# Attention rebuilt in 64-row halves with float32 q and k, inside a float32 attention and two-MLP kernel

## The chip, the cores and the metric

The kernel runs on one core of a Trainium2 chip. The metric is the device time of one launch in microseconds, the median of three runs; lower is better. One execution is also taken by the hardware profiler, and all rows below come from it.

## The reference, cut to what matters

```
# q, k, v: [2, 12, 448, 64] float32
scores = q @ k.T / sqrt(64); scores above the diagonal = -1e9
attn = exp(scores - rowmax); attn /= attn.sum(-1) + 1e-9
x = (attn @ v) -> [2 * 448, 12 * 64]
xn = x / sqrt(mean(x * x, -1) + 1e-6) * rms_g
g = xn @ w_gate; val = xn @ w_val          # [768, 1536] each
y = (g * sigmoid(g) * val) @ w_out         # [1536, 768]
out = relu(y @ w_in) ** 2 @ w_out2         # [768, 2048], [2048, 768]
```

The five weight matrices arrive as float64, the rest as float32. All results are float32.

## The kernel before, in words

TensorE (PE) does every product. To get float32 accuracy out of fast products, each operand is split into a high and a low float32r part, and three products (high x high, high x low, low x high) are summed in PSUM. For the weights the split costs six steps a chunk of 768 columns: `w_exponent`, `w_sign`, `w_upper`, `w_lower` (float64 words to float32), `w_high`, `w_low` (lines 175 to 213). PSUM has eight one-bank buffers in one pool, `ps_m`.

**Attention, lines 232 to 456.** The unit is a head; two heads (a pair) share a load, with head 0 on partitions 0 to 63 and head 1 on 64 to 127. Queries go in four chunks of CP = 112. For a head: `stack` (L299) issues three DMAs on SP's queue that copy the parts of q and k to both partition halves, so that one 128-row product does two of the three split products; `scores` (L309) does one float32 product for chunk 0 (L319, from the raw q and k) and two float32r products for each other chunk (L329: one of 128 rows with `st`, one of 64 rows with `qkl`); `shift` (L331) masks and scales from PSUM to SBUF and takes the row minimum on VectorE (DVE); `expo` (L346) exponentiates on ScalarE (ACT) and sums the rows with the accumulator; `transpose` (L360) turns the weights, ten 112x112 transposes a head; `split_h` and `split_l` (L376, L390) split them on ACT and DVE; `values` (L394) multiplies by v, whose stationary tiles have zeros in the other head's columns (L408, nine float32r products, and one float32 product L403). The sums' reciprocals make a way through DRAM: `over_sums` (L418) writes them, `spread_sums` (L428) reads them back as rows, and `finish` (L413) multiplies. `square` and `add_square` collect RMSNorm's sums. GpSimd (POOL) rounds and splits q, k (`prep_h`, `prep_l`).

**The order around it.** The programs of all engines are in an order written by hand: `BODY` lists the steps of one head with lags, in four phases, and `run` (L605) emits them. From head 23 on, `solo` steps convert the weights of the first five features of the first MLP (SOLO = 5) and `fill` (L549) puts their products for batch 0, 180 products at L552, one by one between attention's. `norm_step` does RMSNorm for each batch after its heads.

**After attention.** `mlp1` (L651): features 5 to 11 and batch 1 of features 0 to 4, whose weights are loaded and converted a second time; each feature has 36 products of 448 columns a batch (L230 to L232 in `mm3`). Then `layer` (L671) for w_out, w_in and the last weights. From the first of these products on there are 2268.

Of the kernel before, what the change touches and what calls it, by code (L numbers as in the profile page):

```python
# [9 lines left out]
F32R = mybir.dt.float32r  # L10
U32 = mybir.dt.uint32
# [7 lines left out]
CP = 112  # L19
# [5 lines left out]
SOLO = 5  # L25
WARM = 9

QB = 2
THREE = 24
KT = [23, 25, 26, 27, 28, 29, 31, 32, 33, 35, 35, 36]  # L30
I0 = -1
PH = [19, 19, 26]
ENG = {'last': 'AAAA',
 'prep_h': 'PAAP',
 'prep_h0': 'D',
 'prep_l': 'PPPP',
 'radd': 'DDDD',
 'split_h': 'AAAA',
 'sqadd': 'PPPP',
 'square': 'PAAP',  # L40
 'v_h': 'AAAA',
 'v_l': 'DPPP',
 'w_exponent': 'APAA',
 'w_high': 'PAPA',
 'w_low': 'DDPP',
 'w_lower': 'DDDD',
 'w_sign': 'DDPD',
 'w_upper': 'DDDD'}
NORM_H = ['APPPPP', 'AAADDD']
NORM_L = ['PPPPDD', 'PPPPDD']  # L50
START = [['load', 1], ['load', 0], ['prep_h', 0], ['v_h', 0], ['prep_l', 0], ['v_l', 0], ['load', 2]]
BODY = [[['load', -4], ['fill', 8], ['heat', 1], ['scores0', -1], ['stack', -2], ['values', 2], ['expo1', 0],
  ['norm', 0], ['finish', 4], ['v_l', 1], ['expo3', 0], ['w_upper', -2], ['shift0', -1], ['fill', 7],
  ['norm', 0], ['tr0', 0], ['w_low', -3], ['sh1', 1], ['prep_h', -4], ['solo_load', 0], ['solo_done', 4],
  ['load_g', 4], ['w_exponent', 1], ['over_sums', 1], ['norm', 0], ['sh2', 1], ['scores2', -1], ['norm', 0],
  ['sl1', 1], ['fill', 5], ['scores1', -1], ['solo_mms', -1], ['fill', 3], ['sl2', 1], ['w_high', 0],
  ['shift2', -1], ['spread_sums', 2], ['scores3', -1], ['shift1', -1], ['square', 4], ['norm', 0],
  ['heat', 3], ['fill', 1], ['tr2', 0], ['expo0', -1], ['shift3', -1], ['sh0', 0], ['norm', 0],
  ['w_lower', -4], ['v_h', 0], ['w_sign', -2], ['add_square', 5], ['prep_l', -4], ['tr1', 0], ['sl0', 0],
  ['expo2', -1], ['fill', 3], ['norm', 0], ['fill', 4]],  # L60
 [ ['expo1', 0], ['values', 2], ['scores0', -1], ['solo_mms', -2],
  ['sl0', 1], ['norm', 0], ['square', 5], ['sl1', 2], ['fill', 1], ['tr0', 1],
  ['fill', 1], ['prep_l', -3], ['fill', 1], ['fill', 1], ['norm', 0],
  ['tr2', 1], ['prep_h', -4], ['fill', 1], ['spread_sums', 3], ['expo2', 1], ['sh0', 1],
  ['norm', 0], ['fill', 1], ['expo0', 0],
  ['add_square', 5], ['w_exponent', -4], ['over_sums', 2],
  ['shift3', 0], ['scores3', -1], ['norm', 0], ['sh2', 1], ['load', -6], ['sl2', 1],
  ['shift0', -1], ['fill', 1], ['shift2', 0], ['fill', 1], ['norm', 0], ['finish', 4],
  ['fill', 1], ['v_l', 1], ['fill', 1], ['w_low', -2], ['fill', 1], ['fill', 1],
  ['shift1', -1], ['fill', 1], ['expo3', 0], ['stack', -2],  # L70
  ['fill', 1], ['w_high', -5], ['fill', 1],
  ['norm', 0], ['solo_load', -7], ['w_upper', -4], ['w_lower', -2],
  ['solo_done', 2], ['scores1', -1],
  ['v_h', 0], ['tr1', 0], ['fill', 1], ['fill', 1],
  ['fill', 1], ['w_sign', 0], ['fill', 1], ['fill', 1],
  ['scores2', -1], ['sh1', 0],
  ['norm', 0], ['fill', 0]],
 [['shift1', 0], ['norm', 0], ['v_l', 1], ['expo3', 0], ['finish', 4],
  ['solo_load', -4], ['add_square', 6],
  ['norm', 0], ['fill', 1], ['norm', 0], ['fill', 1], ['w_lower', -2],  # L80
  ['w_sign', -3], ['sh1', 1], ['load', -5], ['fill', 1], ['tr2', 1],
  ['scores3', -1], ['expo0', 0], ['fill', 1], ['fill', 1], ['values', 2],
  ['norm', 0], ['fill', 1], ['stack', -3], ['w_high', -2],
  ['sh0', 1], ['norm', 0], ['prep_l', -3], ['spread_sums', 3], ['shift2', 0],
  ['sh2', 1], ['expo1', 0], ['over_sums', 2], ['solo_mms', -1], ['prep_h', -5], ['w_low', -2],
  ['norm', 0], ['fill', 1], ['scores0', -1], ['scores1', -1],
  ['fill', 1], ['fill', 1], ['scores2', -1], ['sl0', 1], ['expo2', 0],
  ['fill', 1], ['sl2', 1],
  ['v_h', 0], ['solo_done', 1], ['square', 5], ['fill', 1], ['tr0', 0],
  ['w_exponent', -4], ['norm', 0], ['shift3', -1], ['sl1', 1],  # L90
  ['tr1', 0], ['w_upper', -3],
  ['shift0', -1], ['fill', 0]],
 [ ['scores3', -2], ['fill', 1], ['fill', 1],
  ['w_lower', -2], ['fill', 1], ['sh1', 0], ['tr1', 0], ['w_high', -2],
  ['w_sign', -3], ['norm', 0], ['fill', 1], ['prep_h', -5], ['norm', 0],
  ['shift0', -2], ['over_sums', 1], ['finish', 4], ['w_upper', -3], ['scores1', -2], ['prep_l', -4],
  ['solo_done', 2], ['expo1', 0], ['fill', 1],
  ['square', 5], ['norm', 0], ['solo_mms', -1],
  ['fill', 1], ['sh0', 0], ['w_low', -2], ['fill', 1], ['norm', 0],
  ['shift3', -1], ['sl1', 1], ['fill', 1], ['norm', 0], ['sl0', 1], ['tr0', 0],  # L100
  ['expo3', -1], ['spread_sums', 1], ['values', 1], ['fill', 1], ['sl2', 1],
  ['solo_load', -5],
  ['sh2', -1], ['fill', 1], ['w_exponent', -4], ['fill', 1],
  ['fill', 1], ['fill', 1], ['add_square', 5], ['stack', -2], ['norm', 0], ['fill', 1],
  ['v_h', 0], ['expo2', -2], ['tr2', -1], ['shift2', -2],
  ['scores0', -1], ['load', -5], ['shift1', -2], ['fill', 1],
  ['v_l', 0], ['scores2', -2],
  ['norm', 0], ['expo0', -1], ['fill', 0]]]
NORMPOS = [[124, 127, 135, 137, 138, 142, 144, 143, 143, 150, 152, 152, 155, 143, 155, 158, 157, 160, 167, 166, 170, 174], [215, 222, 229, 241, 243, 246, 249, 256, 275, 275, 250, 299, 308, 295, 311, 315, 313, 326, 348, 326, 333, 342]]


@with_exitstack
def tile_attention_moe_moe2(ctx: ExitStack, tc: tile.TileContext, qk, v, wg, wv, wo, w2i, w2o, rms_g, out):
    """float32 throughout: every product's operands are split exactly into two float32r parts
    (12 significant bits each) and the products of the parts are summed in float32 PSUM.

    qk     [B * NPAIR, P, 2, S]  q and k of each pair of heads, transposed
    v      [B * NPAIR, CP, NCH, 2, D]
    wg, wv [NF1, P, NCC, 2 * P]  stationary tiles, contraction on partitions: float64's words
    wo     [NCC, P, NF1, 2 * P]  # L120
    w2i    [NF2, P, NCC, 2 * P]
# [34 lines left out]
    def EP(name):  # L156
        return E(ENG[name][cur_phase[0]])

# [140 lines left out]
    def stack(u):  # L299
        if u < 2:  # L300
            return
# [449 lines left out]
```

## Time and profile before

| | us |
|---|---|
| median of three runs | 764.91 |
| the three runs | 749.92, 775.11, 764.91 |
| profiled execution: from its first to its last instruction | 733.1 |
| PE busy in it | 694.9 |
| DVE busy | 496.0 |
| POOL busy | 292.4 |
| ACT busy | 156.1 |

The page gives the profiled execution's span, and no time around it: between its span and the three runs' times lie 16.8 to 42.0 us, 31.8 to the median. PE's busy time is not time at its peak: products are pipelined, and an array that runs at the lower of its two clock levels is as busy as one at the higher. PEclk is the granted clock as a share of 2.4 GHz; 0.5 is 1.2 GHz.

### The profile page before, as it was taken

To read this page: it belongs to the slowest core of one execution; us is meant where nothing else is said; L and a number is where in the kernel's file an instruction comes from. 1 tells how busy PE (TensorE), PEld (TensorE's weight loads), DVE (VectorE), ACT (ScalarE), POOL (GpSimd) and SP (SyncE) were. 2 spreads that over 40 slices of the span, in tenths; PEclk is the share of its full clock that TensorE was granted. 3 is DMA by queue.
4 is the path that set the end of the run, shared out by engine and by line. 5 is a ranking of instruction groups with operands and counts; after the bars stand their busy time and mean duration, and the time that the engine had idled before them with its cause. 6 is when DMAs were issued, how large, how long until landed. Compare 5 with 4: busy or idle time off the path is not lost.

```text
span 733.1 us, 8884 instructions
## 1 busy us (share of the span) xinstructions
PE 694.9 (95%) x3199; PEld 589.7 (80%) x3199; DVE 496.0 (68%) x799; ACT 156.1 (21%) x409; POOL 292.4 (40%) x282
## 2 busy tenths in 40 slices
PE   7899898999888888999999899999999999999998
PEld 3566566677677777999997799999999999999997
DVE  5447346447859998888799977557888887445510
ACT  3546346445623300000000000001111110000000
POOL 4322323328666543433454432215565544222210
PEclk6859659559998999999999999999999999999999
DMA  6678977697774224334244454333232323443200
GB/s 163 96 110 109 154 105 115 119 163 104 125 170 143 89 79 147 118 109 151 87 129 138 162 174 133 127 91 125 87 129 87 111 83 109 147 139 120 82 26 25
DMA packets 34860, 85.82 MB, mean 117 GB/s; under 512 B 14400, under 2 KB 20288, under 8 KB 34816
## 3 DMA queue, kind: packets, MB, share of 16 engines
q1 hardware_dynamic: 34816, 85.26, 46.5%
q8 instruction: 25, 0.41, 0.3%
q14 instruction: 19, 0.16, 0.1%
HBM read 72.35 MB, written 2.80 MB: 103 GB/s over the span
## 4 chain that ended last, share of the span: by engine, by line
PE 69%; DVE 12%; DMA 12%; issue 3%; POOL 2%; SPq 1%; ACT 1%; DVEq 0%; POOLq 0%; ACTq 0%
PE py L232 15%; PE py L231 15%; PE py L230 15%; PE s L329 6%; DMA st<-qkl 4%; PE o L408 4%; PE ta L367 3%; DMA wraw<-in_wv 3%; DVE wt L198 3%; DMA rd<-r 2%; DVE wt L203 2%; PE pv L232 2%; DVE wraw L194 2%; PE pv L231 2%; PE pv L230 2%
## 5 line engine op out<-in xcount | busy, mean ns | idle before, releaser
L161 POOL TENSOR_SCALAR whl<-wt 128x768 fp32r<-128x768 f32 (+1 forms) x72 | 66.9, 930 | 111.3 <-PE py L232 93.4
L211 DVE TENSOR_TENSOR whl<-wt,whl 128x768 fp32r<-128x768 f32 (+1 forms) x68 | 67.5, 992 | 48.4 <-POOL whl L161 48.2
L340 DVE CUSTOM_DVE_ANT_0 sm<-s,mask 112x224 f32<-112x224 f32 (+2 forms) x96 | 42.2, 447 | 75.4 <-PE s L329 67.5
L184 POOL TENSOR_SCALAR wt<-wraw 128x768 f32<-128x768 f32 (+1 forms) x68 | 62.7, 922 | 74.4 <-DVE whl L211 46.3
L203 DVE SCALAR_TENSOR_TENSOR wt<-wraw,wt 128x768 uint32<-128x768 uint32 (+1 forms) x80 | 84.5, 1058 | 1.3
L198 DVE SCALAR_TENSOR_TENSOR wt<-wt,wraw 128x768 uint32<-128x768 uint32 (+1 forms) x80 | 81.7, 1022 | 2.3
L194 DVE TENSOR_SCALAR wraw<-wt 128x768 uint32<-128x768 uint32 (+1 forms) x75 | 50.2, 671 | 39.6 <-POOL wt L184 34.1
L232 PE MATMUL py<-y,whl 128*128 128x448 f32 x192 | 70.4, 367 | 0.0
L230 PE MATMUL py<-y,whl 128*128 128x448 f32 x192 | 70.4, 367 | 0.0
L231 PE MATMUL py<-y,whl 128*128 128x448 f32 x192 | 70.4, 366 | 0.0
L232 PE MATMUL py<-hh,whl 128*128 128x448 f32 x192 | 70.1, 365 | 0.0
L230 PE MATMUL py<-hh,whl 128*128 128x448 f32 x192 | 70.1, 365 | 0.0
L231 PE MATMUL py<-hh,whl 128*128 128x448 f32 x192 | 70.1, 365 | 0.0
L351 ACT ACTIVATE p<-sm,nb 112x224 f32<-112x224 f32 (+2 forms) x96 | 50.8, 529 | 44.5 <-DVE nb L340 43.1
L232 PE MATMUL py<-h,whl 128*128 128x448 f32 x144 | 53.3, 370 | 2.4 <-DVE whl L211 2.4
L161 POOL TENSOR_SCALAR hh<-hh 128x448 fp32r<-128x448 f32 x32 | 35.1, 1098 | 49.1 <-DVE hh L698 48.7
L230 PE MATMUL py<-h,whl 128*128 128x448 f32 x144 | 53.3, 370 | 0.0
L231 PE MATMUL py<-h,whl 128*128 128x448 f32 x144 | 53.3, 370 | 0.0
L552 PE MATMUL pg<-x,whl 128*128 128x448 f32 x180 | 46.0, 408 | 7.1 <-POOL whl L211 5.8
L161 POOL TENSOR_SCALAR qkh<-qkraw 128x896 fp32r<-128x896 f32 x11 | 10.6, 961 | 96.3 <-DMA qkraw<-in_qk 52.6
L552 PEld LDWEIGHTS pg<-x,whl 128*128 128x128 f32 x180 | 37.2, 212 | 13.2 <-POOL whl L211 7.5
L232 PE MATMUL pv<-x,whl 128*128 128x448 f32 x114 | 42.7, 374 | 3.4 <-DVE whl L211 3.4
(107 smaller groups left out, 1434.6 us busy)
## 6 DMA issues: line engine op xcount, KB each, us to landing
wraw<-in_wg SPq DMA_DIRECT2D x17, 768.0 KB, 4.4
wraw<-in_wv SPq DMA_DIRECT2D x17, 768.0 KB, 4.3
wraw<-in_w2i SPq DMA_DIRECT2D x16, 768.0 KB, 4.2
wraw<-in_wo SPq DMA_DIRECT2D x12, 768.0 KB, 4.3
wraw<-in_w2o SPq DMA_DIRECT2D x12, 640.0 KB, 4.1
qkraw<-in_qk SPq DMA_DIRECT2D x11, 448.0 KB, 10.1
st<-qkh SPq DMA_DIRECT2D x22, 224.0 KB, 7.5
wraw<-in_w2o SPq DMA_DIRECT2D x6, 768.0 KB, 4.5
```

The costliest lines, as they stand in the source:

```text
L161: eng.tensor_scalar(o, i, 1.0, 1.0, ALU.mult, ALU.mult)
L184: eng.tensor_scalar(e["t"], hi, 2.0 ** -112, 1.0, ALU.mult, ALU.mult)
L194: nc.vector.tensor_scalar(e["s"], e["t"].bitcast(U32), 0x80000000, None, ALU.bitwise_and)
L198: nc.vector.scalar_tensor_tensor(u, u, 3, e["s"], ALU.logical_shift_left, ALU.bitwise_or)
L203: nc.vector.scalar_tensor_tensor(u, lo, 29, u, ALU.logical_shift_right, ALU.bitwise_or)
L211: eng.tensor_sub(e["hl"][:, 1, :n], e["t"].rearrange("p (k n) -> p k n", n=P), e["hl"][:, 0, :n].bitcast(F32))
L230: nc.tensor.matmul(ps, w[:, 0, i], x[:, 0], start=first and i == 0, stop=False)
L231: nc.tensor.matmul(ps, w[:, 0, i], x[:, 1], start=False, stop=False)
L232: nc.tensor.matmul(ps, w[:, 1, i], x[:, 0], start=False, stop=last and i == n - 1)
L329: nc.tensor.matmul(h["s"][c][:, o:o + nn], a, b, start=i == 0, stop=i == len(terms) - 1)
L351: nc.scalar.activation(p, h["m"][c], AF.Exp, bias=h["nb"][:, c:c + 1], scale=-1.0, accum_out=e["sums"][:, u % 2, c:c + 1])
L552: nc.tensor.matmul(o, w, xs[0][i][:, part], start=st_, stop=sp_)
```

## The change

Attention is written anew, and everything in it is emitted by a list scheduler in Python (`Order`) that keeps a model of each engine's time: each step has a due time, the engines that may do it with a cost for each, the steps it follows and the buffers it takes; the step that can start first goes next.

The unit is now a pair. Queries go in chunks of 128 (the last has 64), both heads of a pair in one step: head 0 on PE's rows 0 to 63, head 1 on rows 64 to 127, one product after the other (`sc`). q and k stay float32 and are neither split nor copied; the causal mask is added by bf16 products of constants into PSUM. The scores of a pair lie in two PSUM buffers (`s1`, `s2`, two banks each, and there are two such buffers in all). DVE takes the maxima straight from PSUM (`mx`), ACT exponentiates from PSUM with the scale in the instruction, POOL multiplies the weights by 1/sum while the queries still are on partitions (`ml`; nothing goes through DRAM), PE transposes, ACT or DVE copies to SBUF, and `values` does float32 products, head 0 on PE's columns 0 to 63 and head 1 on 64 to 127. The second product of sums with x is gone: `finish` is a copy.

Features 0 to 2 of the first MLP (NE = 3, six chunks of weights) are converted during attention and kept; their products for batch 0 (108) are steps with due time 1000, so they go where PE has nothing else. After attention come batch 1 of those three features, then features 3 to 11 for both batches: 2340 products. `mm3`, `load_w`, `gated` and `layer` stay.

```diff
-CP = 112
+CP = 64
-SOLO = 5
...
+NE = 3
+STRIDE = 5.0
+SLACK = 0.1
+SWITCH = 0.18
...
+    ps_s = att.enter_context(tc.tile_pool(name="ps_s", bufs=2, space=PSUM))
+    ps_t = att.enter_context(tc.tile_pool(name="ps_t", bufs=1, space=PSUM))
+    ps_o = att.enter_context(tc.tile_pool(name="ps_o", bufs=1, space=PSUM))
+    ps_n = att.enter_context(tc.tile_pool(name="ps_n", bufs=1, space=PSUM))
...
+    order = Order(dict(qk=3, v=NV, s=2, p1=2, p2=2, t=1, pt=2, o=1, n=1, x=9, sq=1, ssq=1, raw=2, wt=3, whl=3,
+                       early=3, tt=2, tu=2, hh=2))
...
+        def sc(buf, o, c, new):
+            def f(e):
...
+                s, n = z[buf], P * (c + 1)
+                qs = slice(c * P, (c + 1) * P)
+                for h in range(2):
+                    nc.tensor.matmul(s[:, h, o:o + n], z["qk"][BOTH[h], 0, qs], z["qk"][BOTH[h], 1, :n],
+                                     start=True, stop=False)
+                for k in range(2):
+                    for h in range(2):
+                        nc.tensor.matmul(s[:, h, o + n - P + k * D:o + n], both[BOTH[h], k], both[BOTH[h], 2 + k, k * D:],
+                                         start=False, stop=k == 1)
...
+        def sc3(e):
...
+            for i, h in ((0, 0), (1, 1), (1, 0), (0, 1)):
+                nc.tensor.matmul(s[BOTH[h], i, 256:480], z["qk"][BOTH[h], 0, qs],
+                                 z["qk"][BOTH[h], 1, i * 224:(i + 1) * 224], start=True, stop=i == 0)
+            for h in range(2):
+                nc.tensor.matmul(s[BOTH[h], 1, 416:480], both[BOTH[h], 0, :D], both[BOTH[h], 2, :D],
+                                 start=False, stop=True)
...
+                if k == 6:
+                    nc.vector.tensor_reduce(z["mx"][:, 6:7], src, mybir.AxisListType.XY, ALU.max)
+                else:
+                    nc.vector.tensor_reduce(z["mx"][:, k:k + 2], src, AX, ALU.max)
...
+                nc.scalar.activation(out_, src, AF.Exp, bias=z["nb"][:, k:k + 1], scale=SC,
+                                     accum_out=z["su"][:, k:k + 1])
...
+        for k, (buf, h, o, n, dst) in enumerate((
+                ("s1", 0, 0, 128, "p1"), ("s1", 1, 0, 128, "p1"), ("s1", 0, P, 384, "p1"), ("s1", 1, P, 384, "p1"),
+                ("s2", 0, 0, 256, "p2"), ("s2", 1, 0, 256, "p2"), ("s2", 0, 256, 448, "p2"))):
...
+                E(e).tensor_scalar(t, t, z["r"][:, k:k + 1], 1.0, ALU.mult, ALU.mult)
...
+            for i in range(4):
+                nc.tensor.transpose(z["t2"][:, 0, i * P:(i + 1) * P], z["p2"][:, 0, i * P:(i + 1) * P], ident)
...
+            for j in range(4):
+                n = S - j * P
+                for h in range(2):
+                    nc.tensor.matmul(z["o"][BOTH[h], j * P:S], z["v"][:, j, h * D:(h + 1) * D],
+                                     z["pt"][:, h, KO[j]:KO[j] + n], start=j == 0, stop=j == 3)
...
+        def finish(e):
+            z["x"] = xrp.tile([P, S], F32, tag="xr", name="xr")
+            copy(e, z["x"], z["o"][:, :S])
...
+        for p in range(NPR):
+            step(p)
+        norm(0, (NPAIR + 2.5) * STRIDE)
+        norm(1, 0.0)
+        for k in range(2 * NE):
+            ahead_steps(k, (5 + 0.9 * k) * STRIDE)
+        for ft in range(NE):
+            ahead_products(ft, 1000.0 + ft)
...
+    for ft in range(NE):
+        mlp1(ft, ahead[2 * ft]["hl"], ahead[2 * ft + 1]["hl"], 1)
+    for ft in range(NE, NF1):
+        g, u = load_w(wg[ft], NCC), load_w(wv[ft], NCC)
         for b in range(B):
             mlp1(ft, g, u, b)
-    for ft in range(SOLO):
-        g, u = load_w(wg[ft], NCC), load_w(wv[ft], NCC)
-        mlp1(ft, g, u, 1)
```

A pair's steps after the change, per kind: ten float32 products for scores (six of 128, 256 and 384 columns, four of 224), 14 bf16 products for masks, 16 transposes, eight value products (448, 320, 192 and 64 columns a head); four maxima over 256, 768, 512 and 448 columns; seven exponentials and seven multiplications over 1984 columns; five copies over 2496 columns; one square and one addition over 448.

## Rows read from the trace of the kernel before

**Rows 1.** Windows: length, busy us (count) PE, PEld, DVE, ACT, POOL; PEclk; DMA; GB/s
```profile
0.00:251.00 251.00, 226.80 (x931) 162.22 (x932) 153.70 (x381) 114.36 (x332) 109.00 (x90) 0.78 0.72 129
...
251.00:319.00 68.00, 61.69 (x288) 54.48 (x287) 59.62 (x73) 5.37 (x11) 29.48 (x31) 0.97 0.33 111
...
319.00:733.00 414.00, 406.39 (x1984) 372.98 (x1982) 282.69 (x347) 36.34 (x67) 153.89 (x162) 1.00 0.34 111
```

**Rows 2.** Windows cut where the granted clock changes, columns as in rows 1
```profile
33.30:53.80 20.50, 18.30 (x54) 12.22 (x55) 8.29 (x26) 7.63 (x25) 6.21 (x5) 0.53 0.85 134
...
53.80:77.70 23.90, 23.17 (x122) 16.17 (x121) 16.51 (x52) 15.47 (x51) 5.51 (x5) 0.97 0.81 117
...
77.70:108.40 30.70, 27.82 (x83) 18.70 (x84) 12.65 (x38) 11.10 (x36) 10.19 (x9) 0.52 0.81 118
...
108.40:128.90 20.50, 18.01 (x95) 12.52 (x94) 12.53 (x40) 12.07 (x39) 8.71 (x7) 0.97 0.79 126
...
128.90:163.00 34.10, 34.10 (x111) 23.92 (x111) 14.82 (x50) 13.48 (x42) 10.20 (x9) 0.52 0.80 136
```

**Rows 3.** Timeline of PE: start, us, engine, line, operation [idle before <-releaser]
```profile
35.51 0.59 PE L329 MATMUL s<-st 128*112 128x336 f32 x1 [2.51 <-DMA st<-qkl]
...
80.58 0.59 PE L329 MATMUL s<-st 128*112 128x336 f32 x1 [3.61 <-DMA st<-qkl]
...
128.59 0.38 PE L329 MATMUL s<-st 128*112 128x336 f32 x1 [2.49 <-DMA st<-qkl]
```

**Rows 4.** Timeline of PE, one head at the lower and one at the higher level
```profile
40.13 0.71 PE L319 MATMUL s<-qkraw 64*112 64x112 f32 x2
...
40.77 2.33 PE L408 MATMUL o<-pt,vz 112*128 112x448 f32 x6
...
49.66 0.71 PE L319 MATMUL s<-qkraw 64*112 64x112 f32 x2
...
112.14 0.45 PE L319 MATMUL s<-qkraw 64*112 64x112 f32 x2
...
112.52 1.33 PE L408 MATMUL o<-pt,vz 112*128 112x448 f32 x6
...
114.58 0.55 PE L367 MATMUL ta<-ident,p 112*112 112x112 f32 x4
...
114.89 0.39 PE L329 MATMUL s<-st 128*112 128x336 f32 x1
...
115.21 0.41 PE L329 MATMUL s<-qkl,st 64*112 64x336 f32 x1
...
117.63 0.45 PE L319 MATMUL s<-qkraw 64*112 64x112 f32 x2
```

**Rows 5.** Groups of instructions, shapes apart: | busy us, mean ns | idle before
```profile
L203 DVE SCALAR_TENSOR_TENSOR wt<-wraw,wt 128x768 uint32<-128x768 uint32 x68 | 74.6, 1099 | 0.9
...
L351 ACT ACTIVATION_READ_ACCUMULATOR p<-sm,nb 112x1 f32 x96 | 18.2, 190 | 0.0
...
L351 ACT ACTIVATE p<-sm,nb 112x448 f32<-112x448 f32 x24 | 16.1, 669 | 13.1 <-DVE nb L340 13.1
...
L340 DVE CUSTOM_DVE_ANT_0 sm<-s,mask 112x448 f32<-112x448 f32 x24 | 15.0, 623 | 12.0 <-PE s L329 11.3 <-ACT p L351 0.7
...
L454 POOL TENSOR_TENSOR ssq<-ssq,sq 128x448 f32<-128x448 f32 x10 | 13.8, 1378 | 0.0
...
L163 ACT CAST pt<-ta 112x448 fp32r<-112x448 f32 x24 | 12.7, 530 | 36.0 <-PE ta L367 35.9
...
L161 POOL TENSOR_SCALAR qkh<-qkraw 128x896 fp32r<-128x896 f32 x11 | 10.6, 961 | 96.3 <-DMA qkraw<-in_qk 52.6 <-DMA st<-qkl 15.8 <-DMA vraw<-in_v 10.7
...
L422 DVE TENSOR_SCALAR r<-sums 112x8 f32<-112x8 f32 x12 | 6.6, 550 | 0.0
...
L449 POOL TENSOR_TENSOR sq<-xr 128x448 f32<-128x448 f32 x7 | 6.5, 934 | 0.0
...
L478 PE MATMUL rb<-dg,ones 112*128 112x112 f32 x16 | 3.2, 362 | 0.2 <-DVE dg L473 0.2
```

More of the change, by code (lines that the diff above doesn't have):

```diff
@@ L24 @@
 NPAIR = H // 2
-SOLO = 5
 WARM = 9
[L28 to L108, printed above, removed]
@@ L428, in spread_sums @@
-    def spread_sums(p):
-        e = pairs[p]
-        d = e["rd"]
-        rb = e["rb"] = at.tile([P, S], F32, tag="rb", name="rb")
-        for i in range(2):
-            row = d[i].rearrange("c p -> (c p)").unsqueeze(0).to_broadcast([D, S])
-            nc.sync.dma_start(out=rb[i * D:(i + 1) * D], in_=row)
-    ssqs = []
-    def square(p):
-        e = pairs[p]
+    ps_s = att.enter_context(tc.tile_pool(name="ps_s", bufs=2, space=PSUM))
+    ps_t = att.enter_context(tc.tile_pool(name="ps_t", bufs=1, space=PSUM))
@@ new lines, in tile_attention_moe_moe2 @@
+    both = atc.tile([P, 4, P], BF16, name="both")
+    nc.vector.tensor_copy(both, half)
+    NV = 3
+    vt = []
+    for i in range(NV):
+        t = atc.tile([P, 4, 2 * D], F32, name=f"vt{i}")
+        nc.gpsimd.memset(t[D:, 3], 0.0)
+        vt.append(t)
+    p2t = []
+    for i in range(2):
+        t = atc.tile([P, 2, 512], F32, name=f"p2t{i}")
+        nc.gpsimd.memset(t[:, 1, S:], 0.0)
+        p2t.append(t)
+    L3 = 1408
+    KO = (0, S, 896, 1344)
+    order = Order(dict(qk=3, v=NV, s=2, p1=2, p2=2, t=1, pt=2, o=1, n=1, x=9, sq=1, ssq=1, raw=2, wt=3, whl=3,
+                       early=3, tt=2, tu=2, hh=2))
@@ L440, in square @@
         b = p // NPAIR
+        z["bx"], z["fi"] = bx, fi
         if p % NPAIR == 0:
[L442 to L454 removed]
@@ L579, in tile_attention_moe_moe2 @@
-    head_f = dict(stack=stack, values=values)
-    for c in range(NCH):
-        for n, f in (("scores", scores), ("shift", shift), ("expo", expo)):
-            head_f[f"{n}{c}"] = lambda u, f=f, c=c: f(u, c)
-    for j in range(3):
-        for n, f in (("tr", transpose), ("sh", split_h), ("sl", split_l)):
-            head_f[f"{n}{j}"] = lambda u, f=f, j=j: f(u, j)
-    pair_f = dict(load=load, prep_h=prep_h, prep_l=prep_l, v_h=v_h, v_l=v_l, over_sums=over_sums, spread_sums=spread_sums,
-                  finish=finish, square=square, add_square=add_square)
@@ L634, in tile_attention_moe_moe2 @@
-    with tc.manual_schedule():
-        heat(WARM)
-        for name, p in START:
-            for q in todo(name, p, NPR):
-                pair_f[name](q)
-        for i in range(I0, NH + 60):
-            cur_phase[0] = sum(i >= q for q in PH)
-            for name, lag in BODY[cur_phase[0]]:
-                run(name, lag, i)
-            if nxt.get("solo_done", 0) == len(solo) and not mms and len(xs[1]) == NCC and nslot[0] > max(NORMPOS[1]):
-                break
+    ahead = [dict() for _ in range(2 * NE)]
@@ new lines, in tile_attention_moe_moe2 @@
+    with tc.manual_schedule():
+        ps = ps_n.tile([P, 512], F32, tag="n", name="warm")
+        for _ in range(WARM):
+            nc.tensor.matmul(ps[:, :256], warm[:, :P], warm, start=True, stop=True)
+        for p in range(NPR):
[6 more added lines that the diff above has]
+            ahead_products(ft, 1000.0 + ft)
+        order.add(30.0, {"S": 2.0}, lambda e: nc.sync.dma_start(out=g_sb, in_=rms_g))
+        order.run()
```

671 lines of the change are left out of this document (353 added, 318 removed).

## The prediction

> **What bounds the kernel now.** I read the windows first, to see which stage the change can touch. The first window ends where `mlp1` begins, at 251 us [rows 1]: attention, both norms and 180 MLP products. From there to the end PE runs 2268 products of one kind in 482 us, at a clock of 0.97 to 1.00; in the last 414 us one takes 406.39 / 1984 = 0.205 us, and PE idles under 2%. That part isn't touched. In the first 251 us PE is busy 226.8 us, but its clock is only 0.78, and no other engine is busy over 154 us. So PE bounds this stage too, and the question is why at a low clock.
>
> Cut at the changes of clock, the stage shows it [rows 2]: the mean is 0.97 in two stretches and 0.52 to 0.53 in three, so PE runs at either 2.4 or 1.2 GHz. In each of the three cases the timeline has an idle PE just before or at the fall, of 2.51, 3.61 and 2.49 us, each waiting for a DMA of `stack` [rows 3]. After it the lower level stays for 20.5, 30.7 and 34.1 us although PE is busy nearly throughout. One head, from one chunk-0 product to the next, costs 49.66 - 40.13 = 9.53 us at 1.2 GHz and 117.63 - 112.14 = 5.49 us at 2.4 GHz [rows 4], a factor of 1.74.
>
> How well did PE use its time? At 2.4 GHz the stage holds 24 x 5.49 = 131.8 us of heads, 180 x 0.205 = 36.9 of MLP products and some 6 for the norms (L478 is half of it [rows 5]): 175 us in 251, a share of 0.70. Without the three waits (8.6 us) and half of the three low stretches (42.7 us) it would be 175 / 200 = 0.875. These two shares are my bounds for what a list of waiting engines gets out of PE.
>
> **The change, PE's part.** The price of a float32 product comes from chunk 0: each is two instructions, 112 columns, 0.64 us for the two at 1.2 GHz and 0.38 at 2.4 [rows 4]. One instruction thus differs by 0.13 us, which is 0.13 x 2.4 GHz = 312 cycles that scale with the clock, 2.8 a column. I read that as two cycles a column for the moving operand and the rest for the weights: four cycles a column for the whole product (an estimate). Four transposes take 0.31 us [rows 4], so one of 128 columns 0.09. A change between 128-row and 64-row products costs: 336 columns take 0.32 us where 336 / 448 x 0.205 = 0.154 would do, so 0.17 us.
>
> For one pair at 2.4 GHz, if the two heads' halves work at the same time: scores of the three full chunks 768 columns x 4 cycles = 1.28 us; the last chunk's four products of 224 columns, two at a time, 0.75; values 1024 x 4 = 1.71; loading weights of 128 or 64 columns 36 times, about 0.64; 14 mask products at 0.03 to 0.08, taken as 0.05, 0.7; 16 transposes 1.4; five switches of array shape 0.85. Sum 7.3 us a pair, against 11.0 for two heads now. If the halves don't overlap, the three streams double (+3.74) and the weights hide under them (-0.64): 10.4 us. No row of before has products alternating between the halves, so both ends stay. I take 7.3: the halves use different rows or columns and different banks or partitions, and nothing in the program makes one wait for the other.
>
> The Trainium skill bears on just this. TensorE: Matmul & The Clock Gate, "Part 3: Packing small matmuls", says that products on different tiles of the array run together, and gives 3.07x for four row tiles, not 4x. No run here shows it yet. By that efficiency, 0.77, two halves would gain 1.53x instead of 2x, an estimate of 8.5 us a pair, and the forecast below would be 18 us later.
>
> PE's sum: 12 x 7.3 = 88, norms 3, the 108 early products 22: 113 us at 2.4 GHz. Stack's DMAs are gone, and with them the one thing that idled PE into the lower level; but the list has short waits everywhere and the start (first load, first pair's chain) idles PE too. I take the middle of the two shares, 0.79: 113 / 0.79 = 143 us for the stage. The bounds give 129 and 161.
>
> **The other engines,** per pair, from mean durations [rows 5]: ACT's seven exponentials cost 0.67 for 448 columns plus a 0.19 read, about 4 us over 1984 columns with overlap. DVE's four maxima are not in the trace; the nearest row is its reduction L340, 0.62 for 448, which gives 2.7; the lower bound is 1984 columns at L203's rate, 768 in 1.10, also about 2.8, so little is open. Small DVE operations on sums and maxima: six of about 0.17 (L422's mean of 0.55 holds delays), 1.1. Five copies at L163's 0.53 for 448: 2.9, on ACT or DVE. POOL's seven multiplications at L161's 0.96 for 896: 2.6, square 0.93, addition 1.38. In all 15.6 a pair, 187 for twelve. Six weight chunks at six steps of about 1.0 to 1.1 each add 38, the norms' twelve tiles at some 2.6 each 31, the early features' gating 11: 267 us over three engines, 89 each if shared evenly. That is below PE's 113, so these hide beside PE if the order overlaps pairs; if not, see the last rival. The price of lost cover: every microsecond a pair's chain adds over PE's time costs 12 us.
>
> **After the stage.** 72 more products of 0.205 follow (108 early instead of 180): +14.8. Weight conversions of the first features happen once and not twice, and PE idles 6.3 us between 251 and 319 [rows 1], part of which goes: -4. So 482 + 14.8 - 4 = 493 us.
>
> Span: 143 + 493 = 636, which is 97 below 733. The median of the runs lies 31.8 above that span; I leave the distance: 764.9 - 97 = **668 us**. By the stage's bounds 654 to 686; as the fastest run of before lies only 17 above the span, and a steadier clock would bring the runs closer to that, the likeliest case reaches down to 635.
>
> **The rivals.** *Halves one after the other.* 12 x 10.4 + 25 = 150 us of PE, / 0.79 = 190, span 683, **715 us**. For it: a float32 product is two instructions with weights each, and nothing shows how they share the array. Against: different rows and banks.
>
> *The lower level for the whole stage.* Half the array at work, transposes and 64-column pieces may never bring the clock back. At the factor 1.74: 12 x 7.3 x 1.74 = 153, + 25 + 5 to start = 183, span 676, **708 us**. For: three stretches stayed low with PE fully busy [rows 2]. Against: each began with an idle wait of 2.5 us or more, and each ended.
>
> *Both together:* 12 x 10.4 x 1.74 + 33 = 250, span 743, **775 us**, within 2%.
>
> *Slower: pairs don't overlap.* A pair's scores fill both score buffers (four banks of eight), so the next pair's can't start until the exponentials have read them, and each engine keeps to an order computed from modelled costs. If that order is wrong enough that one pair's chain ends before the next begins, a pair costs its whole chain: scores 3.4, maxima 2.7, exponentials 4, sums and multiplications 3.5, transposes 1.4, copies 2.9, values 2.1: 20 us. 12 x 20 + 25 + 8 = 273, span 766, **798 us**. It decides from 17 us a pair, where the gain is nil. Against: the two buffers come free one by one, halfway through, and the fixed order of before runs heads every 5.49 us through a chain as long.
>
> **How the numbers follow.** Forecast 0.62; halves one after the other 0.15; low level 0.11; both 0.05; no overlap of pairs 0.07. The first three are faster by over 2%: 0.88; within 2% (750 to 780, about what a measurement of this kernel can tell from no change) 0.05; slower 0.07. The range from 635 to 728 takes in the first three cases with some room.
>
> **What would show it.** Right: `mlp1` begins near 143 us; pairs follow each other every 9 to 11 us; PE's records of head 0 and head 1 overlap, a pair's values taking about 2 us at 2.4 GHz and not 3.4; no wait over 2 us on PE after the first pairs, and granted clock above 0.85 in the stage. The first rival shows as values of 3.4 us at the higher level, the second as a clock near 0.5 throughout, the last as PE idle for most of each pair, waiting for DVE or POOL. The forecast is wrong if the part from `mlp1` on differs from 493 by over 10 us, since the change shouldn't reach it.

## The result, and the profile after

The changed kernel takes **638.06 us** (630.93 to 643.65, four runs) against 767.11 (749.92 to 775.11, four runs) before. The ratio is 0.849, with an interval of 0.825 to 0.873; it compares undisturbed executions alone, so it isn't the quotient of the two medians. 668 was forecast, with a range of 635 to 728.

The profiled execution of after has a span of 629.2 us, 103.9 less than before's. These are its windows, columns as in [rows 1], up to the start of `mlp1` and from shortly behind it to the end:

```profile
0.00:151.20 151.20, 124.66 (x929) 86.06 (x929) 102.06 (x181) 75.58 (x227) 102.02 (x165) 0.95 0.33 97
...
160.00:629.00 469.00, 465.75 (x2299) 431.24 (x2297) 311.35 (x389) 41.15 (x76) 166.04 (x179) 1.00 0.33 107
```

The stage takes 151.2 us instead of 251, though 72 of its early products have moved behind it (14.8 us): like for like it lost 85 us. The part behind it takes 477.9 us for 2340 products, where 482 us were spent on 2268: 18.9 us less, like for like. So 82% of the gain lies where the change was made, and 18% in code that it hardly touched.

The clock in the stage is 0.95 instead of 0.78. Where [rows 2] have three low stretches of 20 to 34 us, after has three short ones, columns as before:

```profile
14.26:21.06 6.80, 6.00 (x34) 3.92 (x34) 5.28 (x10) 2.71 (x9) 6.54 (x11) 0.50 0.26 97
...
51.83:55.25 3.42, 3.42 (x13) 2.07 (x15) 2.16 (x4) 1.93 (x8) 3.25 (x5) 0.50 0.02 5
...
96.20:99.62 3.42, 3.42 (x24) 2.28 (x19) 2.83 (x6) 3.02 (x10) 3.32 (x5) 0.50 0.01 3
```

Each of the three falls stands behind idle time of PE, by 1.6 us at most. On PE's timeline (start, us, line, operation, count, and the idle time before it with what ended it):

```profile
12.69 0.49 PE L328 MATMUL s<-qk 64*128 64x128 f32 x4 [1.98 <-ACT p L389]
...
50.92 0.33 PE L433 MATMUL t<-ident,p 128*128 128x128 f32 x1 [1.51 <-POOL p L418]
51.83 1.75 PE L433 MATMUL t<-ident,p 128*128 128x128 f32 x7 [0.58 <-POOL p L418]
...
95.77 0.84 PE L328 MATMUL s<-qk 64*128 64x256 f32 x4 [2.60 <-ACT p2t L389]
```

The timeline of PE over one pair, in the same form, answers to [rows 4]:

```profile
62.20 1.95 PE L485 MATMUL o<-pt,vt 128*64 128x448 f32 x16
64.08 0.70 PE L328 MATMUL s<-qk 64*128 64x256 f32 x4
64.62 0.25 PE L332 MATMUL s<-both 64*128 64x128 bf16 x4
64.80 0.97 PE L341 MATMUL s<-qk 64*64 64x224 f32 x8
...
67.17 0.90 PE L328 MATMUL s<-qk 64*128 64x384 f32 x4
...
69.69 0.33 PE L433 MATMUL t<-ident,p 128*128 128x128 f32 x1 [1.54 <-POOL p L418]
70.59 1.11 PE L433 MATMUL t<-ident,p 128*128 128x128 f32 x7 [0.58 <-POOL p L418]
71.63 1.95 PE L485 MATMUL o<-pt,vt 128*64 128x448 f32 x16
```

A pair's values, 16 instructions, go from 62.20 to 64.08: 1.88 us, as forecast for halves that work at once ("about 2 us"). A pair's work on PE is about 6.9 us (5.8 from 62.20 to the last scores, 1.0 for eight transposes). But the next pair's values start 9.43 us later, and ahead of them stand two waits for POOL's multiplication. The waits of PE in the stage (line waited for: us in total, times, longest) show that no other wait costs as much:

```profile
PE t L433 <- POOL p L418: 9.8, 16, 1.5
PE s L328 <- ACT p2t L389: 3.2, 2, 2.6
```

POOL's timeline around the second of those two value groups shows an engine without a gap over 0.12 us, and what fills it. L418 multiplies the weights by 1/sum, L404 and L408 make 1/sum (an addition, then a power of -1), L179 and L185 convert MLP weights:

```profile
66.89 0.96 POOL L404 TENSOR_SCALAR r<-su 128x4 f32<-128x4 f32 x1
67.93 1.02 POOL L408 TENSOR_TENSOR r<-r,mone 128x4 f32<-128x4 f32 x1
69.06 2.04 POOL L418 TENSOR_SCALAR p<-p,r 128x128 f32<-128x128 f32 x4
71.07 0.91 POOL L179 TENSOR_SCALAR wt<-wraw 128x768 f32<-128x768 f32 x1
72.07 0.94 POOL L185 TENSOR_SCALAR wraw<-wt 128x768 f32<-128x768 f32 x1
72.98 2.24 POOL L418 TENSOR_SCALAR p2t<-p2t,r 128x256 f32<-128x256 f32 x3
```

By groups (busy us, mean ns of one), a power of four numbers a partition costs POOL a microsecond, more than DVE's maximum over 768 columns:

```profile
L418 POOL TENSOR_SCALAR p<-p,r 128x384 f32<-128x384 f32 x24 | 16.0, 678 | 0.0
...
L364 DVE TENSOR_REDUCE mx<-s 128x2 f32<-128x768 f32 x12 | 11.4, 947 | 0.0
L408 POOL TENSOR_TENSOR r<-r,mone 128x4 f32<-128x4 f32 x10 | 10.6, 1057 | 0.8
```

18 of the 24 reciprocals are on POOL, where the scheduler's cost for the two steps together is 0.4 us. From 20 to 100 us POOL is busy 74.50 of 80 us, PE only 65.22:

```profile
20.00:100.00 80.00, 65.22 (x550) 42.04 (x546) 64.16 (x107) 46.74 (x146) 74.50 (x106) 0.95 0.36 110
```

So while the pairs run, POOL is the fullest engine and PE is not. Behind them it is PE again, with the early MLP products:

```profile
114.00:151.20 37.20, 34.03 (x202) 27.06 (x198) 18.81 (x33) 13.54 (x30) 9.59 (x15) 1.00 0.00 1
```

Behind the stage, before's PE still waits for the first features' conversions and for x:

```profile
PE pv L232 <- DVE whl L211: 3.4, 2, 3.1
PE pg L232 <- DVE whl L211: 2.5, 3, 1.4
PE py L232 <- DVE whl L211: 2.4, 1, 2.4
PE pg L231 <- DVE x L495: 1.4, 1, 1.4
PE pv L230 <- POOL whl L161: 0.6, 2, 0.3
```

and after's has a single wait in 478 us:

```profile
PE pg L225 <- DVE hh L662: 0.7, 1, 0.7
```

### The profile page after: what moved, and what is told of

Same layout as the page of the kernel before. It is cut to its first block, busy times and chain, and to the rows that moved or that the text cites. A ratio compares the mean times of both kernels' runs of the same rounds, so it can differ in the third digit from the quotient of the medians.

```text
span 629.2 us, 8360 instructions
## 1 busy us (share of the span) xinstructions
PE 599.2 (95%) x3269; PEld 525.4 (84%) x3269; DVE 418.0 (66%) x577; ACT 117.8 (19%) x305; POOL 269.0 (43%) x344
## 4 chain that ended last, share of the span: by engine, by line
PE 82%; POOL 11%; issue 3%; DVE 2%; ACT 2%; POOLq 0%; ACTq 0%; DVEq 0%
PE py L226 17%; PE py L225 17%; PE py L227 17%; PE pg L225 4%; PE pv L227 4%; PE pg L227 4%; PE pv L225 4%; PE pv L226 4%; PE pg L226 4%; POOL p L418 3%; PE pgv L640 3%; POOL p2t L418 2%; POOL r L408 2%; PE o L485 1%; ACT p L389 1%
## 5 line engine op out<-in xcount | busy, mean ns | idle before, releaser
L156 POOL TENSOR_SCALAR whl<-wt 128x768 fp32r<-128x768 f32 (+1 forms) x68 | 64.1, 943 | 152.4 <-PE py L227 105.2
L179 POOL TENSOR_SCALAR wt<-wraw 128x768 f32<-128x768 f32 (+1 forms) x69 | 64.0, 929 | 63.7 <-DVE whl L206 47.3
L198 DVE SCALAR_TENSOR_TENSOR wt<-wraw,wt 128x768 uint32<-128x768 uint32 (+1 forms) x70 | 71.8, 1026 | 1.1
L193 DVE SCALAR_TENSOR_TENSOR wt<-wt,wraw 128x768 uint32<-128x768 uint32 (+1 forms) x70 | 67.1, 959 | 4.4 <-POOL wraw L185 2.2
L189 DVE TENSOR_SCALAR wraw<-wt 128x768 uint32<-128x768 uint32 (+1 forms) x65 | 37.2, 573 | 36.8 <-POOL wt L179 36.8
L226 PE MATMUL py<-h,whl 128*128 128x448 f32 x144 | 52.6, 365 | 0.0
L227 PE MATMUL py<-h,whl 128*128 128x448 f32 x144 | 52.6, 365 | 0.0
L225 PE MATMUL py<-h,whl 128*128 128x448 f32 x144 | 52.6, 365 | 0.0
L225 PE MATMUL pg<-x,whl 128*128 128x448 f32 x126 | 46.1, 366 | 0.7 <-DVE hh L662 0.7
L748 DVE TENSOR_TENSOR hh<-hh,hh 128x448 fp32r<-128x448 f32 x32 | 36.6, 1142 | 14.9 <-POOL hh L156 14.9
L225 PE MATMUL pv<-x,whl 128*128 128x448 f32 x126 | 46.0, 365 | 0.0
L226 PE MATMUL pv<-x,whl 128*128 128x448 f32 x126 | 46.0, 365 | 0.0
L227 PE MATMUL pv<-x,whl 128*128 128x448 f32 x126 | 46.0, 365 | 0.0
L227 PE MATMUL pg<-x,whl 128*128 128x448 f32 x126 | 46.0, 365 | 0.0
```

The lines of the kernel that those rows point to most:

```text
L156: eng.tensor_scalar(o, i, 1.0, 1.0, ALU.mult, ALU.mult)
L179: eng.tensor_scalar(e["t"], hi, 2.0 ** -112, 1.0, ALU.mult, ALU.mult)
L189: nc.vector.tensor_scalar(e["s"], e["t"].bitcast(U32), 0x80000000, None, ALU.bitwise_and)
L193: nc.vector.scalar_tensor_tensor(u, u, 3, e["s"], ALU.logical_shift_left, ALU.bitwise_or)
L198: nc.vector.scalar_tensor_tensor(u, lo, 29, u, ALU.logical_shift_right, ALU.bitwise_or)
L225: nc.tensor.matmul(ps, w[:, 0, i], x[:, 0], start=first and i == 0, stop=False)
```

## The experiments

**Why was the clock low before, and why isn't it now?** The prediction had blamed the three waits for `stack`. Three versions of the kernel before test that.

*Before without `stack`*: each split product is 64 rows deep, three a chunk instead of two, as `stack` and `scores` had it for the first two heads only; no DMA stands between.

```diff
-        if u < 2:
+        if u < NH:
```

> The kernel before without the DMAs of stack: every head takes three products of 64 rows for its scores, as the first two heads do already; the result is the same. Theory: the waits for these DMAs start the long stretches at 1.2 GHz, and without them the granted clock of the first 180 us is above 0.9 instead of 0.7, which outweighs three more products a head (about 1.0 us at 2.4 GHz): mlp1 starts at 215 to 240 us instead of 251. Rival: the shape of the products (64 rows, transposes, changes of shape) brings the low level, which comes anyway: clock 0.6 to 0.8, and mlp1 starts at 262 us or later.

Measured: 761.54 us (757.66 to 771.42), ratio 0.995 (0.991 to 0.999). `mlp1` begins at 287.3 in the profiled execution, as the rival had it. Nothing was won, because without a wait PE stayed at 1.2 GHz for the whole window, busy for every microsecond of it (window from 20 to 180 us, columns as in [rows 1], here and in the experiments below):

```profile
20.00:180.00 160.00, 160.00 (x555) 122.81 (x553) 80.82 (x230) 66.64 (x219) 40.85 (x30) 0.50 0.47 48
```

So the theory fell: the level is as low without the waits. Whether they began the three stretches of before stays open, because this edit also brings more 64-row products, which the rival blames.

*Before with float32 scores alone*, no splits of q and k:

```diff
-        if c == 0:
-            nc.tensor.matmul(h["s"][c][:, :n], e["raw"][sl, 0, qs], e["raw"][sl, 1, :n], start=True, stop=True)
-            return
+        nc.tensor.matmul(h["s"][c][:, o:o + n], e["raw"][sl, 0, qs], e["raw"][sl, 1, :n], start=True, stop=True)
+        return
```

> The kernel before with one part of the change alone: every chunk's scores are one float32 product from the raw q and k, so the splits of q and k and the DMAs of stack are gone; the result is the same kind of float32 result. PE's work for a head at 2.4 GHz stays near 5.4 us (1120 columns at four cycles are 1.87 us, in place of 2.3). Theory (a product that streams two cycles a column keeps the array at work for longer stretches, and that is what holds 2.4 GHz): the granted clock of the first 180 us is above 0.9, mlp1 starts at 205 to 230 us and the time falls by 20 to 45 us. Rival (one half of the array at work is too little, as in the run without stack): the clock stays at 0.5 to 0.6 and mlp1 starts at 250 to 290 us, the time within 10 us of before or above.

Measured: 779.47 us (771.26 to 789.46), no faster than before, which took 758.78 to 775.16 beside it; `mlp1` begins at 283.5. Again a full PE at the lower level, from 40 to 220 us:

```profile
40.00:220.00 180.00, 180.00 (x524) 117.75 (x524) 72.82 (x239) 69.86 (x221) 31.73 (x32) 0.50 0.46 52
```

*Before with float32 scores and float32 values*, still head after head in before's order, no splits in attention at all:

```diff
-            for k, (a, b) in enumerate(((0, 0), (0, 1), (1, 0))):
-                ...
+            nc.tensor.matmul(
+                o[i * D:(i + 1) * D, S - n:S], e["vraw"][:, 2 * j + i], t[:, 0, o0:o0 + n].bitcast(F32),
+                start=j == 0, stop=j == 2,
+            )
```

> The kernel before with all of attention's splits gone: scores as in the run with float32 scores, and values as one float32 product a key chunk into the head's half of the columns, from an unsplit copy of the transposed weights; heads, chunks of 112 and the order of the steps stay, and the heads are not in turns. PE's work for a head at 2.4 GHz stays near 5.3 us. Both earlier ideas about the clock fell: float32 scores alone left the kernel before at 1.2 GHz, and keeping the halves apart left the changed kernel at 2.4. What is left of the two kernels' difference on PE is float32 values and the order. Theory (float32 values, the longest stretch of streaming without a break, hold 2.4 GHz): the granted clock of the first 180 us is above 0.9, mlp1 starts at 200 to 230 us, the time falls by 25 to 50 us. Rival (the order: short waits and steps of a pair together): the clock stays at 0.5 to 0.7 and mlp1 starts at 250 us or later.

Measured: **695.31 us** (691.82 to 705.97), ratio 0.903 (0.897 to 0.909). `mlp1` begins at 209.8, as the theory had it; the time falls by more than its 25 to 50 us. The clock from 20 to 180 us is up:

```profile
20.00:180.00 160.00, 148.73 (x669) 87.46 (x667) 75.75 (x230) 84.60 (x269) 50.69 (x44) 0.96 0.74 100
```

One head, from one chunk-0 product to the next on PE's timeline, takes 67.58 - 62.01 = 5.57 us:

```profile
62.01 0.45 PE L322 MATMUL s<-qkraw 64*112 64x112 f32 x2
...
67.58 0.44 PE L322 MATMUL s<-qkraw 64*112 64x112 f32 x2
```

That is what a head of before costs at 2.4 GHz, 5.49, where [rows 4] have 9.53 at 1.2. So this edit saves PE no work; it brings the higher level, and that is 72 of the 129 us between 767 and 638. The edit changes three things of the values at once: they are float32, their stationary tiles have 64 columns instead of 128, and one product stands where three did. Which of them brings the level isn't separated, and float32 values beside the old scores weren't tried.

**Do the halves work at once, and what do the turns bring?** *After with the values, masks and last scores of head 0 first and then head 1's*, nothing else moved:

```diff
-            for j in range(4):
-                n = S - j * P
-                for h in range(2):
+            for h in range(2):
+                for j in range(4):
+                    n = S - j * P
```

> The changed kernel with the two heads' products of a step no longer in turns: all of head 0, then all of head 1, in scores, masks and values; nothing else moves and the result is the same. Theory (halves of the array work at the same time only when their products are next to each other): values go from 1.88 us for 16 instructions at 2.4 GHz to 3.3 to 3.6, a pair costs PE 2.5 to 3.5 us more, about 9.9 instead of 7.3, so PE becomes the bound and the time rises by 15 to 35 us. Rival (the array keeps the halves apart by itself, or POOL's pace hides the loss): under 6 us more.

Measured: 639.16 us (637.52 to 648.47), ratio 0.836 (0.829 to 0.843). On PE's timeline the values take 68.77 - 65.55 = 3.22 us:

```profile
65.55 3.29 PE L484 MATMUL o<-pt,vt 128*64 128x448 f32 x16
68.77 0.71 PE L328 MATMUL s<-qk 64*128 64x256 f32 x4
```

The last chunk's scores stayed as they were (0.81 us from L340 to L343, as after's 64.80 to 65.61): head 1's product starts 13 to 14 ns after head 0's although it stands four instructions behind it. The values look different at first, but there a head has eight instructions, and even they overlap in part. Between 67.05 and 67.20 three of them run, two of head 0's 192 columns and head 1's first, of 448 (count: min/median/max ns, first and last start us; the shapes):

```profile
L484 PE MATMUL o<-pt,vt x3: 326/326/590, 66.9 to 67.0; 128*64 128x192 f32 x2, 128*64 128x448 f32 x1
```

In all twelve pairs head 1's first instruction, the ninth in the program, starts 6 ns after head 0's fifth. So on rows and on columns alike a product started four instructions ahead of its turn, and the values, eight apart, lost because of the distance in the program; that columns need turns and rows don't isn't shown. The Trainium skill, TensorE: Matmul & The Clock Gate, "Part 3: Packing small matmuls", gives 3.07x for four row tiles; the two column halves here gain 3.22 / 1.88 = 1.71x, more than the 1.53x estimated from that efficiency.

The 1.34 us a pair are 16 us in all. Neither expectation has what came of them: `mlp1` begins at 160.5, 9.2 us later than in after, and the profiled execution takes 638.4 us instead of 629.2, with a part behind the stage as long. The four runs take 637.52 to 648.47 against 630.93 to 643.65. From 20 to 100 us PE is fuller than after's 65.22, but runs fewer products (528 for 550):

```profile
20.00:100.00 80.00, 71.27 (x528) 46.24 (x526) 61.65 (x101) 43.08 (x136) 73.13 (x102) 0.98 0.35 107
```

So the slower values filled idle time of PE in part, and pushed early products behind the pairs for the rest.

*After with the halves kept apart*: a mask product over all 128 rows stands between the two heads' scores, and the values go head by head.

```diff
-                for k in range(2):
-                    for h in range(2):
-                        nc.tensor.matmul(s[:, h, o + n - P + k * D:o + n], both[BOTH[h], k], both[BOTH[h], 2 + k, k * D:],
-                                         start=False, stop=k == 1)
+                    nc.tensor.matmul(s[:, h, o + n - P:o + n], full[:, 0], full[:, 1], start=False, stop=True)
```

> The changed kernel with the two heads kept apart on PE: the mask is one product of all 128 rows, put between head 0's and head 1's float32 products of each score step, so that head 1's can't start before head 0's end, and values do all of head 0 before head 1; the result is the same. PE's work for a pair at 2.4 GHz goes from 7.0 to about 11 us. Theory (what holds 2.4 GHz is both halves of the array at work at once; float32 alone, one half at a time, did not): the granted clock between 20 and 100 us falls to 0.5 to 0.75 and mlp1 starts at 200 to 270 us, about where it starts in the kernel before. Rival (the level comes from the scheduled order or the early products, not from the halves): the clock stays above 0.9 and mlp1 starts at 170 to 190 us.

Measured: 687.5 us (682.94 to 692.35), ratio 0.900 (0.891 to 0.908). `mlp1` begins at 203.3, where the theory had 200 to 270 and the rival 170 to 190, but the level is the rival's: PE is the bound again, and its level stayed high, from 20 to 140 us:

```profile
20.00:140.00 120.00, 118.27 (x545) 67.94 (x544) 72.44 (x121) 51.63 (x162) 77.33 (x118) 0.99 0.24 73
```

A pair costs PE 11.94 us (80.44 to 92.38). So the theory on the clock fell, and the overlap that this edit takes away is worth 49 us (the values still overlap in part, in 3.22 us as above): without it PE needs 5 us a pair more, of which the idle time that PE had hides some.

**What sets the pace now?** *1/sum on DVE alone*:

```diff
-        r1 = add(T0 + 4, {"D": 0.25, "P": 0.4}, over(0, 4), ex_[:4])
+        r1 = add(T0 + 4, {"D": 0.4}, over(0, 4), ex_[:4])
```

> The changed kernel with one edit: the reciprocals of the sums may go to DVE alone. In the changed kernel POOL does 18 of the 24 of them, at 1.03 us for the power and 0.3 for the addition, and POOL is busy 102 of the 151 us before the first product of mlp1. Theory: POOL sets the pace of the pairs, so taking some 23 us off it brings mlp1's start from 151 to 131 to 139 us, and the time down by 12 to 20 us. Rival: PE's own work and its waits of short latency set the pace, and POOL's chain is only what happens to be late; then mlp1 starts at 147 us or later and the time falls by less than 5 us.

Measured: 633.63 us (623.82 to 635.82), which isn't clear of after's 630.93 to 643.65. `mlp1` begins at 144.2, 7 us sooner, between the two expectations; but the part behind it takes 487.3 us in the profiled execution and not 477.9, with products that follow each other 2% more slowly (the last section comes back to that). POOL is free for a fifth of the window, and DVE took its place (20 to 100 us):

```profile
20.00:100.00 80.00, 67.00 (x582) 44.15 (x584) 71.86 (x145) 51.62 (x161) 61.93 (x84) 0.96 0.36 110
```

*In addition, the multiplications on POOL or ACT*, as the scheduler finds shorter:

```diff
-            ml_.append(add(T0 + (5 if k < 4 else 8), {"P": P_(n)}, ml(k), [r1 if k < 4 else r2],
+            ml_.append(add(T0 + (5 if k < 4 else 8), {"P": P_(n), "A": A_(n) + 0.1}, ml(k), [r1 if k < 4 else r2],
```

> As the run with the reciprocals on DVE, and the multiplications of the attention weights by 1/sum may also go to ACT. Theory (POOL sets the pace): POOL loses part of its 48 us of multiplications too, pairs come down to PE's 7.3 us and mlp1 starts at 120 to 130 us, the time is 8 to 12 us below that of the run with the reciprocals alone. Rival: with POOL relieved once PE is the bound already, so this edit adds under 4 us.

Measured: 624.95 us (624.22 to 626.06), ratio 0.819 (0.813 to 0.824); 8.7 below the run before, as the theory had it, but for another reason: `mlp1` begins at 145.9, no sooner, where 120 to 130 was expected, and what is shorter is the part behind it (477.9 us again). A miss: POOL's load wasn't what was left. DVE is the fullest engine, with 70 of 80 us, in the same window:

```profile
20.00:100.00 80.00, 67.64 (x590) 44.23 (x587) 70.43 (x143) 51.65 (x164) 58.93 (x79) 0.95 0.37 110
```

*On top of that, truer costs for the scheduler* (`COST` of DVE 0.35 for 0.15, POOL's reciprocal 1.35 for 0.4), so that it gives DVE less:

```diff
-COST = {"D": 0.15}
+COST = {"D": 0.35}
...
+        r1 = add(T0 + 4, {"D": 0.45, "P": 1.35}, over(0, 4), ex_[:4])
```

> As the run with the attention weights' multiplications open to ACT, and the scheduler counts a DVE step 0.35 us dearer (0.15 before) and the power on POOL at what the trace shows, 1.35 us; nothing else changes. In that run DVE is busy 16 to 19.6 of every 20 us from 20 to 100 us. Theory (the pace is set by whichever of DVE and POOL carries most, and ACT has 35% free): copies move to ACT, mlp1 starts 4 to 8 us earlier than the 145.9 of that run. Rival (the order's waits, not any engine's sum, set the pace): within 2 us of it, either way.

Measured: 626.27 us (623.36 to 635.93), `mlp1` at 143.2. The stage is 2.7 us shorter, where the theory had 4 to 8 and the rival under 2, and the time is the same.

*One feature's conversion less for DVE*, on top of the multiplications on POOL or ACT:

```diff
-NE = 3
+NE = 2
```

> As the run with the attention weights' multiplications open to ACT, with two early features instead of three: two of six chunks fewer are converted during attention (about 8 us of DVE, 5 of POOL or ACT), and 36 products move from the stage to after it (7.3 us). Theory (DVE's sum sets the pace of the pairs): mlp1 starts 12 to 16 us earlier than 145.9, 7.3 of it being the moved products, and the time falls by 4 to 8 us. Rival (PE and short waits set it): only the moved products count and the time stays within 2 us.

Measured: **621.53 us** (617.18 to 630.0), ratio 0.812 (0.803 to 0.821). `mlp1` begins at 130.1, 15.8 us sooner, as the theory had it; 7.3 of that are the 36 products moved behind the stage, and 8.5 are gained. The median falls by 3.4, less than the 4 to 8 expected, and the intervals overlap. DVE is as full as it was (72.07 of 80 us in the same window) while pairs pass faster, which fits DVE's weight conversions as the pace; POOL and ACT lost steps too, and this run doesn't separate them.

*And one more*:

```diff
-NE = 3
+NE = 1
```

> As the run with two early features, with one. Two more chunks leave attention and 36 more products (7.3 us) move behind it. Theory (DVE's sum still sets the pace in the pairs): mlp1 starts 9 to 13 us earlier than the 130 of that run, and the time falls by 2 to 5 us from 617 to 624. Rival (with one early feature PE has nothing to do beside batch 1's norm, and the pairs are at PE's pace already): mlp1 starts under 7 us earlier, the time is the same or some us more.

Measured: 636.06 us (627.29 to 638.09). `mlp1` begins at 129.5, hardly sooner, though 36 products fewer stand before it. The rival was right: at the stage's end PE has nothing to do beside batch 1's norm. Its waits show it at the first MLP products:

```profile
PE pg L225 <- ACT x L158: 6.6, 1, 6.6
```

Not all of the 14.5 us more are the edit's: the profiled execution had the slower products of the run with 1/sum on DVE, worth some 9.6 us over its 2412 products.

*Two features with the truer costs*:

```diff
-NE = 3
+NE = 2
...
-COST = {"D": 0.15}
+COST = {"D": 0.35}
```

> Two early features, the attention weights' multiplications open to ACT, and a DVE step counted 0.35 us dearer. Theory (DVE's sum): more copies on ACT take another 2 to 4 us off, the time is 613 to 620 us. Rival (waits of the order): as with two early features alone, within 2 us.

Measured: 619.67 us (619.58 to 627.89), ratio 0.813 (0.807 to 0.820), within 2 us of the same without them, which both expectations allow; `mlp1` begins at 132.6, no sooner. By their medians these two are the fastest versions found.

**Why is the part behind the stage shorter?** *Before with one conversion*: batch 1 of features 0 to 4 goes without its second load and conversion and takes the last feature's weights instead, so this run leaves out the right values of these products and shows their time alone.

```diff
     for ft in range(SOLO):
-        g, u = load_w(wg[ft], NCC), load_w(wv[ft], NCC)
         mlp1(ft, g, u, 1)
```

> The kernel before without the second conversion of the first five features' weights: their products for batch 1 take the last feature's weights instead, so this leaves out ten chunks of conversion and the right values of these products. In the kernel before, the 684 products from mlp1's start to the first product of w_out take 152 us, 0.222 each, where the changed kernel takes 0.203. Theory: the conversions of two chunks for only 36 products kept PE waiting for DVE; without them the 684 products take 140 to 145 us. Rival: the loss comes from the tiles' places or from the clock; 149 us or more.

Measured: one run of 763.4 us; the 684 products took from 285.3 to 436.0, 150.7 us, no less than before's 151. The theory fell. The loss isn't at the second conversions: in that run PE has 48.3 busy us in the first 55 (granted clock 0.94), and all of the 96 us from 340 on. It is the entry that costs: PE waits there 4.0 us for DVE's last step of a conversion (L211) and 2.7 us for x. That conversions for feature 5 haven't run ahead is the likely reason; it isn't shown. After has its first three features in SBUF by then, and its 756 products take 153.3 us without a gap.

## Why the prediction was right, and where it was wrong

**Direction, cause of PE's gain, and the rivals: right.** Halves work at once, pairs overlap, the higher level holds. A pair's PE time, forecast as 7.3 us, is 6.9; the values 1.88 against "about 2". With the halves kept apart a pair costs 11.9, where the rival had 10.4. The rival's span of 683 is near that run's 681.2 by luck: its stage is 13 too short (190 for 203.3) and the rest 15 too long (493 for 477.9). Its 715 lies above the measured 687.5 because of the 31.8 that it adds around the span.

**The stage, 143 forecast, 151.2 measured.** The step that failed here is "below PE's 113, so these hide beside PE". The sum over three engines was near (267 forecast; 102.06 + 75.58 + 102.02 = 280), but it isn't shared evenly: the multiplications may run on POOL alone and cost 4.1 us a pair (16.0 + 13.8 + 9.7 + 9.1 in twelve pairs), not 2.6, and the reciprocals, taken as small DVE operations of 0.17 us, cost POOL 24 us in all. PE's share of the stage, taken as 0.79, is (83 + 3 + 22) / 151 = 0.72. That share came from waits in the old kernel, and had no term for an engine beside PE. Two moves off the full engine bear it out: the reciprocals to DVE, -7 us, and later a third of the early conversions away, -8.5 beyond the moved products.

**The low level's cause: wrong, with the right outcome.** "Stack's DMAs are gone, and with them the one thing that idled PE into the lower level" fell with the run without `stack`: with those waits gone the level was low throughout. Idle time may still begin a low stretch. In before the clock falls at 34.6, 78.9 and 130.1 (the cuts of [rows 2] lie some 1.2 us ahead of that), in or up to 1.6 us behind the three waits, and after's three falls stand behind waits too, for ACT and POOL. But two waits of 1.54 and 0.58 us before 69.69 and 70.59, equal to those at 51, have no fall behind them. What differs is how long it lasts: after is back at 2.4 GHz in 3.4 to 6.8 us, where before took 20 to 34 (and 13 once at its start, 3 to 7 three times behind 200). What brought that is float32 values beside float32 scores, which the prediction didn't count as a cause.

**Behind the stage, "-4": mis-sized.** 18.9 us went, like for like. The prediction counted only part of the 6.3 us of idle time up to 319 us. Before's first 684 products take 151 us, 12 more than after's rate of 153.3 / 756 = 0.2028 gives. The waits shown add up to 10.3 us over the whole part. Of the rest some is the pace of one product, 465.75 / 2299 = 0.2026 us after against 0.2048 in the last window of [rows 1], which no experiment here explains (the last section has more on this pace).

**The 31.8 us around the span: mis-sized, and the largest term.** "I leave the distance" took it for a fixed cost. The runs of the experiments list their spans, and only 1.7 to 1.9 us lie around each. The profiled execution of before was simply a short one: 733.1 us at a mean clock of 0.919, where before's runs in the later comparisons take 756.87 us or more, most of them at 0.85 to 0.88. The clock is part of that and not all of it: four of those runs had 0.90 to 0.94 and still took 758.38 to 762.43 us, and what else differed isn't known. So the stage's 251 us and its clock of 0.78 are the good end for before as well. With the level steady after the change, its median lies 8.9 above the profiled span. The prediction named this ("a steadier clock would bring the runs closer") but put it into the range and not into the forecast. That the forecast of 668 missed the measured 638 by no more is partly luck: two errors in one direction (15 us behind the stage, 23 here) less one in the other (8 in the stage) make the 30 us between 668 and 638.

The forecast's own sign of being wrong, a part from `mlp1` on that "differs from 493 by over 10 us", came: it took 478.

## What to carry to other kernels

When the timed runs lie far above the profiled span, look first at whether the profiled execution had the same clock as they; the distance needn't survive the change. Compare where a stage begins and ends in two profiles before you compare medians: turns that seemed to cost 1 us by the medians cost 9 in the stage. A sum over several engines hides only if the program can share it: list for each engine what it alone may do, and price its smallest operations from a row, because a power of four numbers can cost as much as a pass over 768 columns. And before blaming an idle wait for a low clock, take the wait away and see whether the clock rises.

## What the runs showed of the hardware that was not expected

PE at work for every microsecond of 160 and 180 us stayed at 1.2 GHz where nearly all of attention's scores and values were float32r products, and where the values alone were; with float32 scores and values, these on 64 columns and a third as many, the same order of work ran at 0.96. Why one kind of product brings the higher level and the other doesn't stays open.

Products on two halves of the array overlapped when they stood within four instructions of each other in the program: row halves at that distance started 13 to 14 ns apart, and of column halves eight apart the ninth started with the fifth, in all twelve pairs (values of 3.22 us against 1.88 in turns). Row halves further apart weren't tried.

One product has two lengths, and each profiled execution of the changed kernel and its versions keeps to one of them over its MLP part. Tile `pg` (line, operation, count: min/median/max ns, first and last start) in the profile of after, 365 ns:

```profile
L226 PE MATMUL pg<-x,whl x126: 358/365/369, 151.6 to 300.5; 128*128 128x448 f32 x126
```

and in that of after with 1/sum on DVE, 368:

```profile
L226 PE MATMUL pg<-x,whl x126: 368/368/368, 144.5 to 296.4; 128*128 128x448 f32 x126
```

Starts are 0.2027 and 0.2067 us apart. Over 2340 products that is 9 us, the size of the spread among the runs of one kernel here; that it is the cause of the spread is argued, not shown. Seven of these nine profiles have the shorter one; the two with the longer are the run with 1/sum on DVE and the one with one early feature. The kernel before doesn't keep to one length. Its groups in one execution (busy us, mean ns of one) differ by layer, and why isn't known:

```profile
L230 PE MATMUL py<-hh,whl 128*128 128x448 f32 x192 | 70.1, 365 | 0.0
...
L230 PE MATMUL py<-h,whl 128*128 128x448 f32 x144 | 53.3, 370 | 0.0
```
